# Recurrent cross attention into a three-way maxout layer, on one core: hand-written orders, bank list and queues laid out anew, state reads copied by ScalarE

## The chip, the cores and the metric

The kernel runs on one core of a Trainium2 chip. The core has five engines, each with its own instruction stream: TensorE (PE; its weight loads are shown apart as PEld), VectorE (DVE), ScalarE (ACT), GpSimd (POOL) and SyncE (SP, which here only issues DMAs). They meet through semaphores. The metric is the device time of one execution in microseconds; the median of several runs is compared. TensorE writes its results to eight banks of accumulator memory (PSUM, 2 KB per partition each); VectorE and ScalarE copy them out.

## The reference

Attention between `x` (8 batches, 8 heads, 512 positions, 64 wide) and `state` (32 positions) in both directions, then one feed-forward layer on the joined result:

```python
scores = scale * np.matmul(x, state.transpose(0, 1, 3, 2))
a = np.exp(scores - scores.max(-1, keepdims=True)); a /= a.sum(-1, keepdims=True) + 1e-09
xread = np.matmul(a, state)
scores2 = scale * np.matmul(state, x.transpose(0, 1, 3, 2))
a2 = np.exp(scores2 - scores2.max(-1, keepdims=True)); a2 /= a2.sum(-1, keepdims=True) + 1e-09
sread = np.matmul(a2, x)
tokens = np.concatenate([xread, sread], axis=2)   # then (8 * 544, 512)
h = np.maximum(np.maximum(tokens @ w1, tokens @ w2), tokens @ w3)   # 768 wide
return h @ w_out                                                    # 4352 x 512, float32
```

## The kernel before

`xread` is never formed. Since `xread @ w` is `a @ (state @ w)`, the kernel makes for each batch a matrix G (state times the three W, 2 x 128 rows by 3 x 768 columns) and multiplies the attention weights by it. Inputs are cast to bf16.

For one batch the steps are, with the short names that the order strings use:

- `lx` (or `lxg`, `lxu` by halves of the heads) loads x; `xtd` turns it by a DMA transpose on SP's queue (L245), for batches 0 and 1 `xt` on TensorE (L233) with `xtc` copying it out (L240).
- `sc` makes the scores on TensorE (L258), `ex` the exponentials on ScalarE (L265), `sum` their sums and reciprocals on VectorE (L272, L274), `wt` the product on POOL (L280); `atd` turns the weights a by DMA into aT (L298), for batches 0 and 1 `at`, `atc` on TensorE (L291, L294).
- `pad` lays x out with a column of ones on POOL (L304, L307), `sr` makes the reads of the states (L323), `srs` scales them on VectorE (L333 to L339), `srt` turns them by DMA (L342) and `ap` copies them to their place in `atp` (L347).
- `g`/`gc` make G by slices of 128 columns of each W (batches 0 and 1; L359, L377), `gr`/`grc` by runs of columns (the other batches). A run over 256 columns, or a slice, lies in a tile of two banks; `grc` copies it out at L399, whole or, with two letters, one half on each engine. A run of 256 columns lies in two tiles of one bank (`pgh`, L402).
- `l1` is one of the six slices of layer 1: six matmuls into three banks (L412). `m0` copies the first bank out on ScalarE (L427), `ma` and `mb` take the maximum with the second and third on VectorE (L432, L436). Only then are the banks free for another slice.
- `l2` is a quarter of layer 2, six matmuls into one bank (L443); `l2c` copies it out (L450), `so` stores (L473). In the last stage `l2p`, `l2pc`, `sop` do the same by parts of a quarter (L458, L462, L466), and `sos` stores rows of the state reads (L481).
- `lst`, `stc`, `stt`, `stp` load, cast, turn and place the states; `lw`, `lwo` load the weights by parts, `busy` runs matmuls on zeros, `warm` loads ScalarE's exponential.

A letter at the end of an operation is the engine that does it or the queue that issues it: D VectorE, A ScalarE, P POOL, S SyncE. Loads of x and W are issued by POOL.

Nothing reorders the work: `tc.manual_schedule()` is set, and each engine takes its instructions in the order in which three strings list the operations. FIRST has batches 0 and 1 and the start of batch 2; EACH is performed for b = 2 to 6 and holds, with indices relative to b, layer 1 and 2 of batch b and b - 1 and the attention and G of batch b + 1; LAST has batch 7, the layer for the state reads (batch "s") and the last stores. BANKS names, in order of use, which of the four single banks each single-bank tile takes, PAIRS which of the two two-bank tiles. At the end VectorE compares the sums of the exponentials with bounds (`look`, `flag`, L491 to L503), every engine reads that flag (L589), and a branch (L592) repeats the work in a safer form, which this data does not need.

```python
    for g, h in ((0, 2),) if len(c) == 1 else ((0, 1), (1, 2)):
        copier[c[g]](out=v[:, g:h], in_=p[:, g:h, 0:c1 - c0])
```

are the copies of a two-bank run.

Of the kernel before, what the change touches and what calls it, by code (L numbers as in the profile page):

```python
# [15 lines left out]


FIRST = """
    zero; busy 10; clr 3; lxu 0 0 S; lxg 1 0; lst 0 A; lxg 0 1; clr 1; busy 1; stc 0 D; clr 0; ident;
    lxg 1 1; busy 2; lw 0 2 1; stt 0; lst 1 S; cxu 0 0 D; xones 0; xt 0 0; stp 0 A; busy 2; xt 1 0;  # L20
    xtc 0 0 D; sc 0 0; busy 4; warm; xtc 1 0 D; lw 0 1 2; xt 0 1; sc 1 0; lw 0 4 0; xt 1 1; ex 0 0;
    xtc 0 1 A; sc 0 1; xones 1; sum 0 0; stc 1 P; ex 1 0; lw 1 3 2; xtc 1 1 D; lw 3 5 2; ex 0 1; lw 2 3 1;
    sum 1 0; sc 1 1; stt 1; busy 6; lw 3 6 1; lxg 2 1; wt 0 0 P; ex 1 1; at 0 0; sum 0 1; sr 0; atc 0 0 A;
    clr 2; busy 1; wt 1 0 P; stp 1 A; wt 0 1 P; at 1 0; sum 1 1; at 0 1; wt 1 1 D; g 0 0; lxg 2 0; sr 1;
    atc 0 1 A; srs 1; at 1 1; g 1 0; g 1 1; gc 0 0 A; atc 1 0 D; l1 0 0; atc 1 1 A; ones; g 0 1; gc 1 0 A;
    gc 1 1 D; m0 0 0; gc 0 1 A; xtd 2; l1 1 0; g 0 2; srs 0; m0 1 0; lw 5 6 0; g 1 2; l1 1 1; ma 0 0;
    lw 5 6 2; lw 4 5 0; l1 0 1; pad 2; mb 0 0; g 1 3; gc 0 2 A; m0 1 1; gc 1 2 A; ma 1 0; lxg 3 1; g 0 3;
    l1 0 2; m0 0 1; gc 0 3 A; m0 0 2; l1 1 2; g 0 4; mb 1 0; g 0 5; ma 1 1; l1 0 3; gc 1 3 A; lst 2 A; lwo;
    mb 1 1; l1 1 3; m0 1 2; ma 0 1; g 1 4; gc 0 4 A; g 1 5; m0 0 3; gc 0 5 A; l1 0 5; mb 0 1; ma 0 2;
    m0 1 3; mb 0 2; gc 1 4 A; m0 0 5; l1 1 4; ma 1 2; mb 1 2; ma 0 3; ma 1 3; l1 0 4; mb 0 3; mb 1 3;  # L30
    ma 0 5; mb 0 5; m0 1 4; m0 0 4; gc 1 5 A; sc 2 -; lxg 3 0; ma 1 4; mb 1 4; gr 2 1024 1280; lst 3 S;
    gr 2 0 512; ex 2 -; xtd 3; l1 1 5; ma 0 4; gr 2 512 1024; grc 2 1024 1280 D; lx 4; gr 2 1792 2304;
    mb 0 4; stc 3 P; sum 2 -; grc 2 0 512 A; grc 2 1792 2304 D; stc 2 P; l2 0 2; m0 1 5; l2 0 3;
    gr 2 1280 1792; l2c 0 2 D; wt 2 - P; stt 2; grc 2 1280 1792 A; l2 0 1; grc 2 512 1024 A; ma 1 5; mb 1 5;
    l2 0 0; stp 2 D; stt 3; sr 2; stp 3 A; l2c 0 3 D; so 0 2 4 A; l2c 0 1 D; l2c 0 0 A; srs 2; so 0 0 2 P;
    atd 2;
"""
EACH = """
    gr 1 1792 2304; lx 3; gr 1 0 512; l2 -1 3; sc 1 -; grc 1 0 512 A; pad 1; l2 -1 0; ex 1 -; l1 0 0;
    l2 -1 1; grc 1 1792 2304 D; gr 1 1280 1792; gr 1 1024 1280; srt -2; xtd 2; sum 1 -; l2c -1 3 A;  # L40
    gr 1 512 1024; sr 1; l2c -1 0 A; m0 0 0; l1 0 1; ma 0 0; l1 0 2; l2c -1 1 A; so -1 0 2 A; mb 0 0;
    grc 1 1024 1280 DA; l1 0 3; srs 1; m0 0 1; m0 0 2; ma 0 1; m0 0 3; mb 0 1; wt 1 - P; l1 0 5; m0 0 5;
    l2 -1 2; grc 1 1280 1792 A; grc 1 512 1024 A; ma 0 2; l1 0 4; mb 0 2; ma 0 3; mb 0 3; ma 0 5; m0 0 4;
    mb 0 5; ma 0 4; mb 0 4; l2c -1 2 A; atd 1; ap -2 D; so -1 2 4 P;
"""
LAST = """
    srt 7; srt 5; l1 7 0; l2 6 3; l1 7 2; ap 5 A; l2 6 1; srt 6; l1 7 3; m0 7 0; ma 7 0; mb 7 0; ap 6 A;
    ap 7 D; m0 7 2; l2c 6 3 D; l2c 6 1 A; l1 7 4; m0 7 3; l1s 0; m0 7 4; ma 7 2; mb 7 2; ma 7 3; mb 7 3;
    l1 7 1; l2 6 0; m0 s 0; ma 7 4; m0 7 1; l2c 6 0 A; ma s 0; mb 7 4; ma 7 1; mb s 0; mb 7 1; l1 7 5;
    m0 7 5; l1s 2; ma 7 5; mb 7 5; m0 s 2; l2p 7 1 384 512; l1s 1; ma s 2; l2p 7 0 384 512; l2p 7 3 256 512;  # L50
    l2pc 7 1 384 512 A; l2 6 2; m0 s 1; sop 7 1 384 512 S; l2p 7 3 0 256; ma s 1; l2p 7 2 128 384;
    l2pc 7 0 384 512 D; l1s 5; l2pc 7 3 256 512 A; l2c 6 2 A; l2p 7 0 0 128; mb s 2; l1s 3; l1s 4; mb s 1;
    l2pc 7 2 128 384 D; m0 s 5; l2p 7 2 0 128; l2p 7 2 384 512; l2p 7 0 128 256; l2pc 7 3 0 256 A;
    l2p 7 1 0 128; m0 s 3; look; ma s 5; sop 7 3 256 512 S; l2pc 7 0 0 128 D; sop 7 2 128 384 S; m0 s 4;
    sop 7 0 384 512 S; mb s 5; sop 7 0 0 128 A; ma s 3; so 6 2 3 P; so 6 1 2 S; so 6 3 4 S; so 6 0 1 P;
    l2pc 7 2 0 128 A; ma s 4; mb s 3; l2p 7 0 256 384; mb s 4; l2pc 7 0 128 256 D; flag; l2p s 0 0 256;
    l2pc 7 2 384 512 A; sop 7 0 128 256 S; sop 7 2 384 512 S; l2pc 7 1 0 128 A; l2pc 7 0 256 384 D;
    l2pc s 0 0 256 D; sop 7 2 0 128 S; l2p 7 1 128 384; l2 s 1; sop 7 1 0 128 A; l2c s 1 D;
    l2pc 7 1 128 384 A; sop 7 3 0 256 S; sop 7 0 256 384 S; sop s 0 0 256 S; sop 7 1 128 384 S;
    l2p s 0 256 512; l2pc s 0 256 512 D; sos 1 A; sop s 0 256 512 S;  # L60
"""

BANKS = """
    0123012130 2310231031 3232132013 2013210321 0321302301 3203123013 0212302131 2031203120 3123013203
    1201320132 0132013210 3120132031 2031203120 3123013203 1201320132 0132013210 3120132031 2031203120
    3123013203 1201321032 0132013021 0230213021 0320323102 3021320130 120312013
"""
PAIRS = """
    0101010110 1010100010 1010010100 1010010100 10
"""  # L70


# [1 line left out]
def kernel(  # L74
# [10 lines left out]
    nc = tc.nc  # L85

    B, H, S, D = x.shape
# [35 lines left out]
    zero = const.tile([128, 512], BF16, name="zero")  # L123
    ident = const.tile([128, 128], BF16, name="ident")
    ones = const.tile([128, 128], BF16, name="ones")
    warm = const.tile([128, 1], F32, name="warm")
# [3 lines left out]
    flag = data.tile([128, 1], I32, name="flag")  # L130

    xT, e, a, aT, G, ht, osb, xp = {}, {}, {}, {}, {}, {}, {}, {}
# [176 lines left out]
    srs = {}  # L309
# [188 lines left out]
    def set_flag():  # L498
# [3 lines left out]
        nc.vector.reduce_sum(out=n, in_=p, axis=AX.X)  # L502
        nc.vector.tensor_scalar(out=flag, in0=n, scalar1=255.5, scalar2=None, op0=ALU.is_le)  # L503

# [9 lines left out]
        "gr": (g_run, 1), "grc": (g_ran, 1), "l1": (layer1, 1), "l1s": (layer1_states, 0),  # L517
        "m0": (max_first, 1), "ma": (max_second, 1), "mb": (max_third, 1), "l2": (layer2, 1), "l2c": (layer2_out, 1),
        "l2p": (layer2_part, 1), "l2pc": (layer2_part_out, 1), "sop": (store_part, 1), "so": (store, 1), "sos": (store_states, 0), "look": (look_at_sums, 0), "flag": (set_flag, 0),
    }  # L520

    def value(t):
# [38 lines left out]
    def sread_below_max(b):  # L561
# [18 lines left out]
        for g in range(2):  # L580
            p = bank([128, 2, 2, 128], BF16, "pat")
            for c in range(2):
                for i in range(2):
# [2 lines left out]
                           in_=p.rearrange("p i c k -> p (i c) k"))  # L586
        sread(b)

    bad = nc.values_load(flag[0:1, 0:1], min_val=0, max_val=1,  # L589
                         skip_runtime_bounds_check_because="flag is the result of a comparison")  # L590
    homes["b"], homes["w"] = cycle("0123"), cycle("01")
    with tc.If(bad != 0, label="again"):  # L592
        for b in range(B):
# [68 lines left out]
```

## Time and profile before

| | us |
|---|---|
| median of 3 runs (lowest, highest) | 156.79 (156.53, 157.11) |
| span of the profiled execution | 155.3 |
| TensorE busy in it | 147.1 |
| VectorE busy | 113.6 |
| ScalarE busy | 87.1 |
| GpSimd busy | 52.1 |

The span reaches from the first to the last thing that the profiler recorded; a run's time has about 1.5 us around it. Lines of the profile give start and length in us, then engine, source line, operation, output and inputs with partitions x elements; `xN` counts instructions in a row, and a bracket gives the idle time before and what ended it. The granted TensorE clock is a share of full speed. The stretches of the windows view are columns of busy time by engine.

### The profile page before, as it was taken

Reading aid. Unit: us, or ns where it says so; the run is one execution under the profiler, and the core shown is the slowest. Engines: PE = TensorE matmul, PEld = TensorE weight load, DVE = VectorE, ACT = ScalarE, POOL = GpSimd, SP = SyncE. Lnnn points to the kernel's source line nnn. Section 1 sums busy time; section 2 is a strip of 40 time slices with the busy share of each in tenths; the row PEclk is TensorE's granted clock in tenths of the full one; section 3 lists DMA queues with packets and bytes.
Section 4 is the critical chain, followed back from the end, with each engine's and each line's share of the span. In section 5 each row is a group of like instructions: output and inputs, shape, how many; then the busy total and the mean of one; then the engine's idle time right before and its main releaser. Section 6 shows DMA issues by size and latency. Waiting matters only on the chain.

```text
span 155.3 us, 3610 instructions
## 1 busy us (share of the span) xinstructions
PE 147.1 (95%) x1429; PEld 73.6 (47%) x1429; DVE 113.6 (73%) x196; ACT 87.1 (56%) x143; POOL 52.1 (34%) x69
## 2 busy tenths in 40 slices
PE   6989899999999999999999999999999999999960
PEld 2565333354453444444444443444344445679930
DVE  3577788799957788877687799688978767636530
ACT  0677787865486476557655865466637543333300
POOL 6999509502239007700770073106220100002000
PEclk9999999999999999999999999999999999999995
DMA  4999999999979996998499930923060300015444
GB/s 123 231 196 201 196 189 171 159 189 196 194 194 224 268 151 200 130 178 163 153 128 179 177 135 0 174 44 135 4 211 17 135 2 4 0 37 202 167 145 142
DMA packets 39477, 22.30 MB, mean 144 GB/s; under 512 B 23584, under 2 KB 37408, under 8 KB 39456
## 3 DMA queue, kind: packets, MB, share of 16 engines
q0 software_dynamic: 14944, 10.75, 40.5%
q1 hardware_dynamic: 22928, 7.47, 28.2%
q10 hardware_dynamic: 1584, 3.80, 6.8%
q8 instruction: 12, 0.20, 0.5%
q14 instruction: 9, 0.07, 0.2%
HBM read 15.20 MB, written 8.91 MB: 155 GB/s over the span
## 4 chain that ended last, share of the span: by engine, by line
PE 77%; DVE 9%; DMA 6%; POOL 4%; issue 1%; DVEq 0%; POOLq 0%
PE pw L412 45%; PE po L443 19%; DMA w<-in_moe_w_dram 6%; PE pg L359 5%; PE po L458 4%; DVE atp L347 3%; DVE ht L436 2%; PE psr L323 2%; DVE seen L272 1%; DVE G L399 1%; POOL x L166 1%; PE ps L258 1%; POOL w L177 1%; DVE t L432 1%; POOL x L194 1%
## 5 line engine op out<-in xcount | busy, mean ns | idle before, releaser
L412 PE MATMUL pw<-aT,G 128*128 128x512 bf16 x288 | 67.1, 379 | 0.0
L432 DVE TENSOR_TENSOR t<-t,pw 128x512 bf16<-128x512 bf16 (+1 forms) x54 | 35.0, 649 | 14.4 <-ACT t L427 11.8
L427 ACT CAST t<-pw 128x512 bf16<-128x512 f32 (+1 forms) x54 | 30.6, 567 | 23.8 <-PE pw L412 19.9
L412 PEld LDWEIGHTS <-G 128*128 128x128 bf16 x288 | 27.2, 98 | 33.6 <-issue 2.7
L443 PE MATMUL po<-wout,ht 128*128 128x512 bf16 x168 | 40.6, 379 | 0.0
L436 DVE TENSOR_TENSOR ht<-t,pw 128x512 bf16<-128x512 bf16 x48 | 32.9, 686 | 4.8 <-PE pw L412 0.5
L473 POOL DMA_DIRECT2D out_dram<-osb x8 | 4.8, 601 | 66.1 <-ACT osb L450 43.4
L443 PEld LDWEIGHTS <-ht 128*128 128x128 bf16 x168 | 15.3, 98 | 19.3 <-issue 2.3
L399 ACT CAST G<-pg 128x1024 bf16<-128x1024 f32 x18 | 17.7, 1019 | 4.6 <-PE pg L359 4.6
L450 ACT COPY osb<-po 128x512 f32<-128x512 f32 x24 | 13.6, 589 | 10.9 <-PE po L443 10.9
L280 POOL TENSOR_TENSOR a<-e,rden 128x1024 bf16<-128x1024 bf16 (+1 forms) x9 | 14.6, 1636 | 14.4 <-DVE rden L274 6.5
L307 POOL COPY xp<-x 128x1024 bf16<-128x1024 bf16 x12 | 12.4, 1071 | 5.3 <-DMA x<-in_x_dram 5.3
L359 PE MATMUL pg<-w,bd 64*32 64x512 bf16 (+1 forms) x288 | 12.2, 364 | 0.6 <-DMA w<-in_moe_w_dram 0.6
L272 DVE TENSOR_REDUCE seen<-e 128x32 f32<-128x1024 bf16 (+1 forms) x10 | 9.9, 990 | 3.5 <-ACT e L265 3.5
L265 ACT ACTIVATE e<-ps 128x1024 bf16<-128x1024 f32 (+1 forms) x10 | 8.4, 853 | 4.0 <-PE ps L258 2.9
L377 ACT CAST G<-pg 128x768 bf16<-128x768 f32 x11 | 8.9, 808 | 2.9 <-PE pg L359 2.9
L207 PE MATMUL idle<-zero 128*128 128x512 bf16 x26 | 8.5, 472 | 1.3 <-DVE zero L185 1.3
L412 PE MATMUL pw<-atp,w 128*128 128x256 bf16 x72 | 8.7, 273 | 0.0
L359 PEld LDWEIGHTS <-bd 64*32 64x32 bf16 x336 | 3.5, 89 | 9.0 <-issue 7.6
L177 POOL DMA_DIRECT2D w<-in_moe_w_dram x10 | 7.6, 773 | 0.4 <-DMA w<-in_moe_w_dram 0.4
L412 PEld LDWEIGHTS <-w 128*128 128x128 bf16 x72 | 7.0, 98 | 1.2
L347 DVE COPY atp<-ats 128x128 bf16<-128x128 bf16 x6 | 7.5, 1254 | 0.0
(66 smaller groups left out, 111.2 us busy)
## 6 DMA issues: line engine op xcount, KB each, us to landing
out_dram<-osb ACTq DMA_DIRECT2D x6, 512.0 KB, 5.0
out_dram<-osb POOLq DMA_DIRECT2D x6, 512.0 KB, 3.0
x<-in_x_dram POOLq DMA_DIRECT2D x4, 512.0 KB, 8.1
x<-in_x_dram POOLq DMA_DIRECT2D x7, 256.0 KB, 5.9
w<-in_moe_w_dram POOLq DMA_DIRECT2D x3, 256.0 KB, 9.2
wout<-in_moe_w_out_dram POOLq DMA_DIRECT2D x1, 768.0 KB, 9.4
out_dram<-osb SPq DMA_DIRECT2D x6, 128.0 KB, 3.0
w<-in_moe_w_dram POOLq DMA_DIRECT2D x5, 128.0 KB, 8.4
```

Of the source, the lines that this page charges most:

```text
L272: nc.vector.reduce_sum(out=den, in_=parity(e[b], g), axis=AX.X)
L280: times[c](out=parity(a[b], g).rearrange("p j g s n -> p j (g s) n"), in0=parity(e[b], g).rearrange("p j g s n -> p j (g s) n"), in1=rdens ...
L307: nc.gpsimd.tensor_copy(out=xp[b][:, :, :, g * (D + 1):g * (D + 1) + D], in_=v[:, g])
L347: copier[c](out=atp[:, :, b // 4, :, b % 4], in_=ats[:, b])
L359: nc.tensor.matmul(p(s, g), bd(b, 2 * s + g)[64 * g:64 * g + 64, g, :], f(w_sb[64 * g:64 * g + 64, s]), start=True, stop=True, tile_positi ...
L399: copier[c[g]](out=v[:, g:h], in_=p[:, g:h, 0:c1 - c0])
L412: nc.tensor.matmul(pw[i][:, 0:n], lhs(i, k), rhs(k), start=(k == 0), stop=(k == nk - 1))
L427: nc.scalar.copy(out=t0s[b, m][:, 0:n], in_=open_ps["l", b, m][0][:, 0:n])
L432: nc.vector.tensor_max(t1s[b, m][:, 0:n], t0s.pop((b, m))[:, 0:n], open_ps["l", b, m][1][:, 0:n])
L436: nc.vector.tensor_max(ht[b][:, m, :], t1s.pop((b, m))[:, 0:n], open_ps.pop(("l", b, m))[2][:, 0:n])
L443: nc.tensor.matmul(p, ht[b][:, m, j * 128:(j + 1) * 128], wout_sb[:, m, :], start=(m == 0), stop=(m == NM - 1))
L450: copier[c[i]](out=o[:, j, i * w:i * w + w], in_=p[:, i * w:i * w + w])
```

## The change

Only orders, the bank and pair lists and one small function change; what is computed stays. The passes:

```diff
 EACH = """
-    gr 1 1792 2304; lx 3; gr 1 0 512; l2 -1 3; sc 1 -; grc 1 0 512 A; pad 1; l2 -1 0; ex 1 -; l1 0 0;
-    l2 -1 1; grc 1 1792 2304 D; gr 1 1280 1792; gr 1 1024 1280; srt -2; xtd 2; sum 1 -; l2c -1 3 A;
-    gr 1 512 1024; sr 1; l2c -1 0 A; m0 0 0; l1 0 1; ma 0 0; l1 0 2; l2c -1 1 A; so -1 0 2 A; mb 0 0;
-    grc 1 1024 1280 DA; l1 0 3; srs 1; m0 0 1; m0 0 2; ma 0 1; m0 0 3; mb 0 1; wt 1 - P; l1 0 5; m0 0 5;
-    l2 -1 2; grc 1 1280 1792 A; grc 1 512 1024 A; ma 0 2; l1 0 4; mb 0 2; ma 0 3; mb 0 3; ma 0 5; m0 0 4;
-    mb 0 5; ma 0 4; mb 0 4; l2c -1 2 A; atd 1; ap -2 D; so -1 2 4 P;
+    pad 1; l2 -1 0; gr 1 1792 2304; gr 1 1024 1280; l2c -1 0 A; grc 1 1024 1280 DA; gr 1 0 512; l1 0 0;
+    l2 -1 3; l1 0 1; m0 0 0; ma 0 0; sc 1 -; grc 1 0 512 AD; m0 0 1; mb 0 0; grc 1 1792 2304 AD; ma 0 1;
+    l2 -1 1; l1 0 2; ex 1 -; sr 1; l2c -1 1 A; mb 0 1; gr 1 1280 1792; gr 1 512 1024; l1 0 3; m0 0 2;
+    so -1 0 2 A; srt -2; l1 0 5; l1 0 4; sum 1 -; m0 0 3; m0 0 5; l2 -1 2; l2c -1 3 D; ma 0 2; srs 1;
+    mb 0 2; ma 0 3; m0 0 4; mb 0 3; ma 0 5; mb 0 5; grc 1 512 1024 DA; wt 1 - P; ap -2 A; ma 0 4;
+    mb 0 4; l2c -1 2 D; so -1 2 4 P; lx 3; xtd 2; grc 1 1280 1792 A; atd 1;
 """
```

In a pass, the load of x and its transpose move to the end, three runs of G are copied by halves (one on ScalarE, one on VectorE), two of the four copies of layer 2 move from ScalarE to VectorE, and the copy of the state reads moves from VectorE to ScalarE. In FIRST and LAST (cut):

```diff
 FIRST = """
-    zero; busy 10; clr 3; lxu 0 0 S; lxg 1 0; lst 0 A; lxg 0 1; clr 1; busy 1; stc 0 D; clr 0; ident;
...
+    lxg 0 1; lxg 1 0; zero; clr 0; busy 1; busy 2; lxu 0 0 S; clr 1; ident; busy 1; lxg 1 1; busy 1;
+    busy 1; busy 1; lst 0 A; stc 0 D; busy 1; busy 1; stt 0; xones 1; cxu 0 0 D; stp 0 D; xt 0 0;
+    busy 1; lw 0 4 0; xtc 0 0 A; lw 0 1 2; busy 2; busy 1; xones 0; xt 0 1; busy 2; xtc 0 1 D; sc 0 0;
+    ex 0 0; xt 1 0; sc 0 1; lst 1 S; busy 1; busy 1; busy 1; xtc 1 0 AD; xt 1 1; busy 1; ex 0 1;
+    sum 0 0; sum 0 1; busy 1; xtc 1 1 AD; lw 0 2 1; lw 1 3 2; sc 1 0; lw 2 3 1; busy 1; sr 0; sc 1 1;
+    busy 1; ex 1 0; ex 1 1; busy 1; wt 0 0 P; at 0 0; busy 2; sum 1 0; wt 0 1 P; sum 1 1; wt 1 0 P;
+    busy 2; at 0 1; atc 0 0 A; at 1 0; lw 5 6 0; srs 0; busy 1; stc 1 A; stt 1; g 1 0; wt 1 1 D;
+    lw 5 6 2; lw 3 5 2; atc 0 1 A; g 0 0; lw 3 6 1; at 1 1; sr 1; atc 1 0 A; gc 1 0 D; g 0 1; g 1 1;
+    srs 1; gc 0 0 A; l1 0 0; gc 0 1 D; lw 4 5 0; atc 1 1 A; gc 1 1 A; stp 1 DA; m0 0 0; g 0 2; g 1 2;
...
+    ma 1 2; gc 1 4 AD; g 0 5; xtd 2; m0 0 3; g 1 5; l1 1 3; mb 1 2; gc 0 5 A; l1 0 5; m0 1 3; ma 0 3;
...
+    grc 2 1024 1280 AD; l2 0 2; m0 1 5; gr 2 0 512; xtd 3; srs 2; gr 2 1792 2304; so 0 0 2 P;
+    grc 2 512 1024 AD; ma 1 5; atd 2; stp 3 AD; mb 1 5; l2c 0 2 D; grc 2 1792 2304 A; grc 2 0 512 DA;
+    lx 4; so 0 2 4 S;
 """
...
 LAST = """
-    srt 7; srt 5; l1 7 0; l2 6 3; l1 7 2; ap 5 A; l2 6 1; srt 6; l1 7 3; m0 7 0; ma 7 0; mb 7 0; ap 6 A;
...
-    l2p s 0 256 512; l2pc s 0 256 512 D; sos 1 A; sop s 0 256 512 S;
+    l1 7 2; srt 5; ap 5 D; l1 7 0; srt 6; l1 7 3; m0 7 2; m0 7 0; srt 7; l1 7 4; ap 6 A; ma 7 2; mb 7 2;
...
+    l2p s 0 256 512; sop 7 2 128 384 P; sop 7 3 256 512 A; sos 1 A; l2pc 7 0 128 256 D;
+    l2pc s 0 256 512 A; sop s 0 0 256 P; sop s 0 256 512 A; l2pc 7 0 384 512 D; vl; sop 7 0 384 512 P;
+    sop 7 0 128 256 S;
 """
...
+    bads = []
+
+    def read_flag():
+        bads.append(nc.values_load(flag[0:1, 0:1], min_val=0, max_val=1,
+                                   skip_runtime_bounds_check_because="flag is the result of a comparison"))
...
+        "vl": (read_flag, 0),
...
-    bad = nc.values_load(flag[0:1, 0:1], min_val=0, max_val=1,
-                         skip_runtime_bounds_check_because="flag is the result of a comparison")
+    bad = bads[0]
```

In FIRST the G slices, layer 1 slices and maxima of batches 0 and 1 stand next to each other slice by slice, the weights are loaded in another order, the warm-up matmuls are 28 instead of 26 in more and smaller groups, and some copies go to another engine. In LAST the layer 2 parts and stores come in another order, POOL and ScalarE issue more of the stores (all DMAs: ScalarE 15 for 11, POOL 34 for 30, SyncE 9 for 17), and the flag is read ahead of the last two stores (`vl`).

## The prediction

> **What bounds it now.** I read the page's busy shares, then the chain of waits, then the busy time of each engine cut at the passes (cut points are the starts of the first G run of each pass), then the timeline where a pass is long.
>
> ```profile
> PE 147.1 (95%) x1429; PEld 73.6 (47%) x1429; DVE 113.6 (73%) x196; ACT 87.1 (56%) x143; POOL 52.1 (34%) x69
> ```
>
> TensorE works in 95% of the span and no other engine comes near. The change leaves its matmuls alone (1429 against 1431), so a gain can come only from its waits, the head (first slice of layer 1 starts at 17.02) and the tail. The passes, columns being length, then busy time of PE, PEld, DVE, ACT, POOL:
>
> ```profile
> 43.60:58.85 15.25, 15.25 (x157) 6.89 (x164) 10.72 (x19) 10.76 (x18) 5.48 (x6) 1.00 1.21 216
> 58.85:74.10 15.25, 15.25 (x157) 6.83 (x164) 12.36 (x20) 9.70 (x16) 5.61 (x6) 1.00 0.95 170
> 74.10:89.35 15.25, 15.25 (x157) 6.84 (x164) 11.56 (x20) 9.70 (x16) 5.51 (x6) 1.00 0.88 159
> 89.35:105.51 16.16, 15.88 (x156) 6.80 (x164) 13.32 (x20) 9.70 (x16) 4.63 (x5) 1.00 0.39 85
> ```
>
> Three passes are pure TensorE work, 15.25 each at clock 1.00. The fourth is 0.91 longer with the same work. The chain of waits (start, length, what) shows why, and the timeline (start, length, engine, line, operation) shows what the long piece is:
>
> ```profile
> 89.35 0.60 PE pg L359 x16
> 89.95 0.67 DVE ht L436
> 90.62 2.16 DVE atp L347
> 92.78 1.04 DVE G L399
> ```
> ```profile
> 75.29 0.30 DVE L347 COPY atp<-ats 128x128 bf16<-128x128 bf16 x1
> ...
> 90.54 2.24 DVE L347 COPY atp<-ats 128x128 bf16<-128x128 bf16 x1
> 90.56 2.05 POOL L307 COPY xp<-x 128x1024 bf16<-128x1024 bf16 x2
> ...
> 96.66 0.42 DVE L402 CAST G<-pgh 128x256 bf16<-128x256 f32 x1
> 96.69 0.37 ACT L402 CAST G<-pgh 128x256 bf16<-128x256 f32 x1 [0.41 <-PE pgh L359]
> ```
>
> The same small VectorE copy takes 0.30 alone and 2.24 beside POOL's padding copies; VectorE then runs late and TensorE waits for banks. It happens again at 106.7, costing about 0.44. So the waits in the passes come to 0.91 + 0.44 = 1.35 us: all that the passes have to give.
>
> **The change, part by part.**
>
> *State reads copied by ScalarE (ap).* The VectorE copies of 2.13 to 2.24 go; ScalarE's two of this kind take 0.486 each. No row has one beside POOL's copies: from 0.49 (ScalarE's other copies there, 0.59 and 1.01, keep their usual time) to 2.24. I take 0.49; ScalarE is busy 9.7 of 15.25. Gain 1.35. At 2.24, up to 1.75 a pass, ScalarE's idle time still covers it.
>
> *Halves.* In EACH three of the four two-bank G pieces (0-512, 1792-2304, 512-1024) are now copied half by ScalarE and half by VectorE ("AD", "DA"). By sizes the pair looks like 0.59 and 0.68 side by side in place of 1.02. But the program as built has, on the second engine's copy, a wait on the first engine's counter, since both read one two-bank tile; the 256-wide pieces, two separate tiles, have none, and the rows at 96.66 and 96.69 run together. So a split piece takes 0.59 + 0.68 = 1.27 in series, where the whole took 1.02 on ScalarE (two of the three) or 1.21 on VectorE (1792-2304). What is queued behind the second copy waits too: VectorE's max operations, which free layer 1's banks.
>
> *VectorE also gets* two of four layer 2 copies (0.684 each) and loses the atp copy. By rows a pass of VectorE is 12 max operations 8.20, three halves 2.05, a 256 half 0.42, sum 1.57, two layer 2 copies 1.37, state-read scaling 0.46: 14.07, where it had 10.7 to 12.4. That still fits a pass; the order decides.
>
> *Order in a pass.* T = 0 is the start of layer 1's slice 1. Its first bank is done at 0.59, ScalarE's m0 runs 0.69-1.28, its half of 1792-2304 1.18-1.76 (an engine starts its next work some 0.1 before the last ends), VectorE's half 1.80-2.49, then ma 2.40-3.08 and mb 3.18-3.87. TensorE, after layer 2 of the batch before and the scores, wants slice 2's banks at 3.05: it waits 0.08 and 0.36. Next on VectorE: the reduction 3.79-5.00, reciprocal 5.04-5.39, layer 2 copy 5.31-6.00, ma of slice 2 5.91-6.59. TensorE wants slice 3 at 5.79: 0.48 in three waits. The last mb ends at 12.37 and the next pass begins with a layer 2 that needs it: 0.18. Together 1.10 a pass, for five passes 5.5. In the first place VectorE's half waits for ScalarE's; the layer 2 copy in the second is one that ScalarE had.
>
> *Entry to the passes.* VectorE does two ma/mb pairs in a row (0.68 + 0.69 + 0.69 + 0.69) ahead of its half of the 0-512 piece of batch 2, and ScalarE's half waits behind that: TensorE wants the pair's banks at 45.69 and gets them at 46.67, 0.98, with 0.19 before it. In the last stage the same form costs 0.10 and 0.58 (m0 7 2 behind a half, an ap 0.49 and a G copy 1.02). Entry and end: 1.85.
>
> *Head.* The x part of batch 0 that needs a cast still lands at 4.90 and the cast ends at 5.63. From there: transposes to 6.37, ScalarE's copy (1.01 where VectorE takes 0.69) to 7.42, second half copied by 8.41, scores 8.63, exps to 8.98; batch 1's xT halves in series (0.58, then 0.41), exps, the first sum to 10.48, its reciprocal to 10.77. POOL's three products:
>
> ```profile
> 11.13 3.10 POOL L280 TENSOR_TENSOR a<-e,rden 128x512 bf16<-128x512 bf16 x3
> ...
> 16.73 0.36 PE L359 MATMUL pg<-w,bd 64*32 64x384 bf16 x8 [0.59 <-DMA w<-in_moe_w_dram]
> ```
>
> run 10.91-14.07 instead, and transposes with a state turn (0.22) put the first G at 14.96, before 14.61: +0.35. After that the slices of both batches stand side by side and wait for halves (placing of states, gc 1 4) and banks: 0.36, 0.28, 0.09, 0.09, 0.08 and 0.36, and 0.2 for the second G piece of batch 0: 1.46 to 1.6 where before had 0.92 (0.59 of it the wait for W in the row above, which the new W order removes or not: 0 to 0.59). I carry +1.1 at batch 2's scores. Warm-up matmuls (26 to 28) lie in time in which TensorE waits anyway; the VectorE/ScalarE chain of the head hides them, and uncovered they would be 2 x 0.47.
>
> *Fewer G visits and a moved state turn* save TensorE 0.36 of switching (entering a G visit costs 0.09, leaving about 0.3, by gaps between rows).
>
> *Tail.* Before, POOL's last store is issued by 141.6 and landed at 143.98, and SP's last is issued at 151.06, 1.8 behind the last matmul group's start:
>
> ```profile
> 149.28 0.82 PE L458 MATMUL po<-wout,hts 128*128 128x256 bf16 x6
> ...
> 151.06 0.56 SPq L466 DMA_DIRECT2D out_dram<-osb  x1
> ```
>
> Now POOL issues stores to the very end. POOL's closing steps, in the trace's raw records, start when its stores have landed: 0.79 and a drain of 2.51, hidden before. Last store issued about 0.3 behind the last copy, landing 2 later, 0.1 + 0.79 + 0.03 + 2.51 + 0.83: 6.6 to 7.1 from the last matmul's start to the end, before 155.30 - 149.82 = 5.48: +1.2 (0 if the drain overlaps the landings, +1.6 at most). The flag's read, ahead of the last two stores, lies beside the waits for copies: nothing, at most one store's issue, 0.6.
>
> **Sum**: +1.1 (head) + 5.5 + 1.85 (waits) - 1.35 - 0.36 = +6.8 for the last matmul; +1.2 tail; +8.0. The profiled span of 155.3 becomes 163.3. The median of the runs, 156.79, has 1.5 outside that span: 164.8.
>
> **Rivals.**
>
> (A) *The halves run side by side*, the wait being satisfied early or absent. For: the rows at 96.66 and 96.69. Against: the built wait, 18 such halves. With the half at 0.68 beside 0.59, five passes and the entry lose about 5.2 less: 159.6. The Trainium skill, PSUM — Partial Sum Buffer, section "PSUM bank collisions raise a hardware error", has two engines on different banks run clean, which speaks for the chip not needing this wait; by that rule alone the time would be this rival's, but the program's wait is there whatever the chip needs.
>
> (B) *The DMA chain x, xT, a, aT becomes the bound.* The load of x and the transposing DMA move to the end of the pass. In my pass the sum ends at 5.39, POOL's product (1.91) at 7.4, and aT is wanted about 13.85: 6.4 for a transfer whose rows land in 2.7 to 5.95; at 5.4 with its issue there is 0.85 to spare. Landing 1.5 later costs (1.5 - 0.85) x 5.5 = 3.6: 168.4. For: rows near 6. Against: less DMA traffic on SP (9 issues against 17). The Trainium skill, SBUF — State Buffer, section "Who interferes with whom", says a VectorE copy can hold up POOL's making of descriptors; more VectorE copies and 34 POOL DMAs against 30 would push this way, and no row here shows an issue so stretched.
>
> (C) *Faster*: VectorE's lag stays inside the bank slack (TensorE never waits in the passes), the 1.35 goes, the 0.36 too, and head and tail come out even: 156.79 - 1.71 = 155.1. It decides if VectorE's half and the max behind it end before 3.05 in the pass, which needs halves side by side and the reduction elsewhere. For: three passes had no wait at 12.36 of VectorE work. Against: 14.07 of it now.
>
> That the change does nothing measurable: the head's and tail's losses just meet the 1.35. It needs (C)'s passes too.
>
> **How the numbers follow.** Forecast 0.62 (its own range 162 to 167.5: tail 0 to 1.6, head 0.5 to 1.5, a pass 0.7 to 1.5); A 0.17; B 0.12; C 0.06; even 0.03. A measurement here can tell 0.5%, 0.8 us, from no change. Faster 0.06, same 0.03, slower 0.91. The range must reach A at 159.6 and half of B: 159.5 to 168.5, leaving out C, even and B's upper half, some 0.15.
>
> **What would show it.** Passes near 16.3, all alike, with TensorE waiting for ma, mb; "AD" copies ending one behind the other; atp copies of 0.5 on ScalarE; first G near 15.0; the span's end 6.6 or more behind the last matmul. It is wrong if passes stay near 15.3 (A, C), if TensorE waits for aT by DMA (B), or if POOL's end is hidden again.

## The result, and the profile after

The changed kernel takes 167.38 us (median of 4, 166.84 to 167.87), the kernel before 156.83 in the same comparison: ratio 1.0666, 95% interval 1.0634 to 1.0697. It is slower by 10.5 us, and the spans of the two profiled executions differ by as much (165.77 - 155.30 = 10.47). All ratios rest on the faster executions of a kernel, and the profiled ones of three kernels further on (separate banks, whole copies, last POOL stores on SyncE) lie 1.5% or more above the fastest of theirs. The busy shares of the page after:

```profile
PE 150.1 (91%) x1415; PEld 73.7 (44%) x1431; DVE 118.7 (72%) x217; ACT 81.5 (49%) x143; POOL 53.6 (32%) x72
```

TensorE's share falls from 95% to 91%: the work is the same and the waits have grown. Its busy time still rises, from 147.1 to 150.1, because the record of a layer matmul lasts 0.38 while the next one usually starts 0.22 behind it: the first 0.16 of a wait counts as busy. Two marks that both traces have, the start of batch 2's scores and the start of the last matmul, cut the loss in three:

| stretch (us) | before | after | difference | in the prediction's sum |
|---|---|---|---|---|
| to batch 2's scores | 33.93 | 37.18 | +3.25 | +1.1 |
| from there to the last matmul | 115.89 | 120.26 | +4.37 | 5.5 + 1.85 - 1.35 - 0.36 = +5.64 |
| from there to the end of the span | 5.48 | 8.33 | +2.85 | +1.2 |

The windows view, cut at the scores of four passes after the change (length; busy time of PE, PEld, DVE, ACT, POOL; clock; DMA share; GB/s):

```profile
53.32:69.46 16.14, 15.78 (x149) 6.79 (x148) 12.91 (x22) 8.76 (x16) 5.51 (x6) 1.00 0.58 126
69.46:85.60 16.14, 15.73 (x147) 6.78 (x148) 12.91 (x22) 8.70 (x16) 5.51 (x6) 1.00 0.78 148
85.60:101.74 16.14, 15.73 (x147) 6.80 (x148) 12.91 (x22) 8.71 (x16) 5.51 (x6) 1.00 0.83 150
101.74:117.96 16.22, 15.75 (x148) 6.80 (x149) 12.91 (x22) 8.72 (x16) 4.62 (x5) 1.00 0.62 142
```

Three of these are 16.14 and the last is 16.22, at full clock: at least 0.89 more than the 15.25 of an undisturbed pass before, though no engine is full. The chain of waits in one of them (start, length, what):

```profile
68.33 0.45 PE pw L415 x2
...
68.85 0.58 ACT t L430
69.44 0.50 ACT G L402
...
69.96 0.69 DVE G L402
70.65 0.60 DVE t L435
...
71.35 0.69 DVE ht L439
72.03 1.14 DVE seen L275
...
73.47 0.64 DVE osb L453
...
74.15 3.99 PE pw L415 x17
```

For 5.3 us the chain leaves TensorE: ScalarE's m0 and its half of a G run, then VectorE's half, which starts as ScalarE's ends, then the maxima, the sum and the layer 2 copy that VectorE got, until a bank comes free at 74.11. TensorE has other work for most of that time, but not for all of it: by the starts of its matmuls it loses 0.44 at layer 1's slice 2 and 0.33 at slice 3. A third and smaller wait stands in the first layer 2 of the next pass, which needs the last mb:

```profile
80.50 0.11 PEld L446 LDWEIGHTS <-ht 128*128 128x128 bf16 x2 [0.49 <-DVE ht L439]
```

The two matmuls around it start 0.38 apart and not 0.22: 0.16.

At the head the timeline has a wait that the kernel before has not, on a transfer:

```profile
27.07 4.43 SPq L248 DMA_TRANSPOSE xT<-x  x1
...
37.18 0.64 PE L261 MATMUL ps<-bd,xT 128*128 128x64 bf16 x16 [1.55 <-DMA xT<-x]
```

Further on stands the wait that the prediction has at the entry to the passes, for the pair of banks whose second half ScalarE copies after VectorE:

```profile
49.08 0.41 PE L362 MATMUL pg<-w,bd 64*32 64x512 bf16 x8 [0.97 <-ACT G L402]
```

### The profile page after: what moved, and what is told of

The parts are those of the page before. It is cut to its first block, busy times and chain, and to the rows that moved or that the text cites. A ratio compares the mean times of both kernels' runs of the same rounds, so it can differ in the third digit from the quotient of the medians.

```text
span 165.8 us, 3624 instructions
## 1 busy us (share of the span) xinstructions
PE 150.1 (91%) x1415; PEld 73.7 (44%) x1431; DVE 118.7 (72%) x217; ACT 81.5 (49%) x143; POOL 53.6 (32%) x72
## 4 chain that ended last, share of the span: by engine, by line
PE 50%; DMA 14%; DVE 14%; ACT 8%; POOL 5%; issue 4%; POOLq 0%; DVEq 0%; ACTq 0%; SPq 0%
PE pw L415 28%; PE po L446 14%; DMA xT<-x 6%; DMA x<-in_x_dram 5%; DVE G L402 3%; ACT G L402 3%; DVE ht L439 2%; DMA osb<-in_x_dram 2%; ACT t L430 2%; DVE osb L453 2%; POOL w L180 2%; DVE t L435 2%; DVE seen L275 2%; PE po L461 2%; PE pg L362 2%
## 5 line engine op out<-in xcount | busy, mean ns | idle before, releaser
L415 PE MATMUL pw<-aT,G 128*128 128x512 bf16 x288 | 69.8, 379 | 2.6 <-DVE ht L439 1.2
L446 PE MATMUL po<-wout,ht 128*128 128x512 bf16 x154 | 39.7, 379 | 0.7
L402 ACT CAST G<-pg 128x512 bf16<-128x512 f32 (+1 forms) x24 | 17.6, 733 | 7.4 <-DVE G L402 6.1
L402 DVE CAST G<-pg 128x512 bf16<-128x512 f32 x17 | 11.7, 685 | 7.2 <-ACT G L402 7.2
L476 POOL DMA_DIRECT2D out_dram<-osb x7 | 4.3, 609 | 30.9 <-DVE osb L453 18.9
L362 PE MATMUL pg<-w,bd 64*32 64x512 bf16 (+1 forms) x288 | 11.5, 364 | 1.0 <-ACT G L402 1.0
L453 DVE COPY osb<-po 128x512 f32<-128x512 f32 x15 | 10.0, 666 | 3.2 <-PE po L446 3.2
L453 ACT COPY osb<-po 128x512 f32<-128x512 f32 x14 | 8.1, 586 | 8.2 <-PE po L446 8.2
L210 PE MATMUL idle<-zero 128*128 128x512 bf16 x26 | 9.0, 466 | 1.4 <-DVE zero L188 1.3
L471 POOL DMA_DIRECT2D out_dram<-osb x4 | 2.2, 540 | 22.8 <-ACT osb L465 21.7
```

The costliest lines, as they stand in the source:

```text
L362: nc.tensor.matmul(p(s, g), bd(b, 2 * s + g)[64 * g:64 * g + 64, g, :], f(w_sb[64 * g:64 * g + 64, s]), start=True, stop=True, tile_positi ...
L415: nc.tensor.matmul(pw[i][:, 0:n], lhs(i, k), rhs(k), start=(k == 0), stop=(k == nk - 1))
L446: nc.tensor.matmul(p, ht[b][:, m, j * 128:(j + 1) * 128], wout_sb[:, m, :], start=(m == 0), stop=(m == NM - 1))
L453: copier[c[i]](out=o[:, j, i * w:i * w + w], in_=p[:, i * w:i * w + w])
```

## The experiments

Each of the twelve kernels below was timed beside the kernel before. "Ratio" is to that, with its 95% interval, and a time given with a ratio is the ratio times 156.83. The wait for the head's transfer is 0.9 to 3.9 in the profiles of the kernels that keep it, and the three named above had 2.9 to 3.9. So a part is read from its own stretch of the trace as well: scores of batch 2 to last matmul is 120.26 in the changed kernel.

**Separate banks for the halves.** Each two-bank tile becomes two tiles of one bank (orders and engines stay; scores, slices and runs of G likewise). With that, a whole copy of two banks becomes two copies, and the exponentials go in two instructions:

```diff
-    def two_banks(shape, dtype, name):
-        return pp.tile(shape, dtype, tag="w" + next(homes["w"]), bufs=1, name=name)
+    def two_tiles(shape, dtype, name):
+        w = next(homes["w"])
+        return [pp.tile(shape, dtype, tag=f"w{w}{h}", bufs=1, name=f"{name}{h}") for h in range(2)]
```

> The changed kernel (167.4) with each two-bank tile replaced by two tiles of one bank, so that a half on the second engine no longer waits for the half on the first; same engines, same orders (the exponentials go in two instructions). Theory S (the wait between the two halves, in series, is most of the loss in the passes): TensorE's first stall of a pass (0.44) goes and the second shrinks, passes 16.14 become about 15.4, the 0.97 at the entry goes: 162 to 163. Rival V (the copies that VectorE got, by their mere length and order, are the loss): halves overlap in the trace, but the passes stay above 15.9 and the time at 166 or more.

Measured: ratio 1.0262 (1.0226 to 1.0297), 160.9 on 156.83. Passes 15.36, TensorE's list of waits empty from 54 to 116; scores to last matmul 116.40. One pass, and the halves in its timeline:

```profile
70.01:85.37 15.36, 15.26 (x147) 6.81 (x148) 13.10 (x23) 8.72 (x18) 5.51 (x6) 1.00 0.82 156
```

```profile
53.87 0.68 DVE L410 CAST G<-pg 128x512 bf16<-128x512 f32 x1
54.04 0.59 ACT L435 CAST t<-pw 128x512 bf16<-128x512 f32 x1 [1.52 <-PE pw L420]
54.52 0.59 ACT L410 CAST G<-pg 128x512 bf16<-128x512 f32 x1
```

VectorE copies its half while ScalarE is still busy with m0, and no longer waits for ScalarE's. VectorE is as busy in a pass as in the changed kernel (13.1, there 12.9), so it is not its load by itself that cost. Theory S holds, and V falls. The stretch is 3.86 shorter, the time 6.4. The rest is not in the passes. A shorter wait at the head in the executions behind the ratio would give at most 1.55 of it, and the tail in the trace is 0.27 shorter; some 0.8 stays open, and no trace of those executions is at hand.

**Whole copies in the passes.** The same question from the other side:

```diff
-grc 1 0 512 AD; ... grc 1 1792 2304 AD; ... grc 1 512 1024 DA;
+grc 1 0 512 A;  ... grc 1 1792 2304 D;  ... grc 1 512 1024 A;
```

> The changed kernel with the three split runs of G in a pass copied whole again by the engines of before (0-512 and 512-1024 ScalarE, 1792-2304 VectorE), nothing else. Theory S: VectorE's copy no longer waits 1.2 for ScalarE, its first max starts 0.65 earlier, both stalls of a pass (0.4 each) go: passes 15.3 to 15.4, entry wait stays: about 163.3. Rival V: VectorE loses 0.84 of 14 us a pass and no more than that can come back; if the layer 2 copy on VectorE is what holds the banks, one stall of 0.4 stays: passes 15.7 to 15.8, 165.3.

Measured: ratio 1.0326 (1.0274 to 1.0378), 161.9. Passes 15.27, scores to last matmul 115.42, 4.84 less than the changed kernel and 0.47 less than before the change; the entry's 0.97 stays. One pass:

```profile
72.01:87.28 15.27, 15.16 (x147) 6.82 (x148) 12.41 (x21) 8.96 (x14) 5.51 (x6) 1.00 0.83 157
```

VectorE still has its two layer 2 copies of a pass here, so the stall behind them needs the late start that the halves cause. Whole copies do better in this stretch than halves in separate tiles (115.42 against 116.40, there with every whole copy in two as well): here the split wins nothing even when its halves need not wait for each other.

**Layer 2 copies on ScalarE again**, one of them further ahead in the order.

```diff
-l2c -1 1 A; ... l2c -1 3 D; ... l2c -1 2 D;
+l2c -1 3 A; l2c -1 1 A; ...     l2c -1 2 A;
```

> The changed kernel with VectorE's two layer 2 copies of a pass on ScalarE again. Theory S: the second stall of a pass (0.4, behind VectorE's layer 2 copy) goes, the first (behind the serial halves) stays: passes 15.7, about 165.2. Rival V: both go, passes 15.3, about 163.

Measured: ratio 1.0705 (1.0632 to 1.0777), no gain in time; the scores of batch 2 came at 38.30 in its profile, 1.1 later than in the changed kernel's. In the trace the passes are 15.86: 0.28 less, where S said 0.4 and V 0.8.

```profile
70.30:86.17 15.87, 15.57 (x148) 6.89 (x149) 11.82 (x20) 9.44 (x18) 5.51 (x6) 1.00 0.82 152
```

The timeline has the same wait between the halves as the changed kernel, and the first stall; no wait for VectorE's layer 2 copy is left in the list of waits of the passes:

```profile
86.67 0.69 DVE L402 CAST G<-pg 128x512 bf16<-128x512 f32 x1 [1.19 <-ACT G L402]
...
88.80 1.02 PE L415 MATMUL pw<-aT,G 128*128 128x512 bf16 x4 [0.20 <-DVE ht L439]
```

So it points to S, with a smaller second stall than worked out: the layer 2 copies on VectorE cost 0.28 a pass, and only behind the serial halves. Scores of batch 2 to last matmul took 119.16, 1.10 less; in the profiled execution the head took as much, and the times don't show it.

**x of batch 2 loaded early.** POOL's queue, behind the first three products:

```diff
-at 1 0; lw 5 6 0; ... lw 5 6 2; lw 3 5 2; ... lw 3 6 1; ... lw 4 5 0; ... lxg 2 1; mb 0 0; lxg 2 0;
+lw 3 5 2; lw 3 6 1; lw 4 5 0; lxg 2 1; lxg 2 0; lw 5 6 0; lw 5 6 2;
```

> The changed kernel with the load of x of batch 2 put before two parts of W in POOL's queue (behind the first three products), so that it lands about 2 to 3 us earlier. Theory D (scores of batch 2 wait 1.55 for the turned x, because its load stands behind five loads of W and its transpose then runs beside the load of the output weights for 10 us): the transpose starts near 24, lands by 34 to 35, the wait goes: 165.8, with scores of batch 2 near 35.6. Rival: behind that wait is another of the same length, a bank that VectorE or ScalarE holds, and the time stays within 0.5 of 167.4.

Measured: ratio 1.0572 (1.0544 to 1.0600), 165.8; scores of batch 2 at 35.38. Theory D holds to 0.3, though the transpose took 9.4 here too: what helped is that it began 2.5 earlier. The four times lie within 0.53 of each other.

**Last POOL stores on SyncE.**

```diff
-so 6 1 2 P; ... sop 7 0 0 128 P; ... sop 7 2 128 384 P; ... sop s 0 0 256 P; ... sop 7 0 384 512 P;
+so 6 1 2 S; ... sop 7 0 0 128 S; ... sop 7 2 128 384 S; ... sop s 0 0 256 S; ... sop 7 0 384 512 S;
```

> The changed kernel with the last five stores that POOL issues moved to SyncE's queue. Theory P (POOL ends with about 0.87 and a drain of 2.84 that start only when its last store has landed, exposed here): from the last matmul's start to the span's end 8.4 becomes 5.5, as before the change: 164.5. Rival F (reading the flag ahead of the last stores delays them): the end stays 7 or more behind the last matmul, 166.5 or more.

Measured: from the last matmul to the end 5.39, against 8.33: theory P holds to 0.1. The ratio, 1.0546 (1.0480 to 1.0612), shows 1.9 less and not 2.9, with a wide interval: in its profiled execution the scores of batch 2 waited 3.9 for the head's transfer.

**Flag read last.** `vl` is put behind the last store.

> The changed kernel with the flag read behind the last two stores instead of ahead of them. Theory P: nothing, within 0.4 of 167.4. Rival F: 1 us or more is won.

Measured: ratio 1.0720 (1.0685 to 1.0755), the end 8.32 behind the last matmul. Nothing is won, and F falls.

**x and its transpose in the front half of a pass.**

```diff
-so -1 2 4 P; lx 3; xtd 2; grc 1 1280 1792 A;
+lx 3; l1 0 1; ... srt -2; xtd 2; l1 0 5; ... so -1 2 4 P; grc 1 1280 1792 A;
```

> The changed kernel with the load of x and its transpose put back into the front half of a pass. Theory: they have time to spare in the passes either way, within 0.4 of 167.4. Rival B (the chain of DMAs bounds the passes): 1 us or more is won.

Measured: ratio 1.0641 (1.0584 to 1.0698), passes 16.14, scores to last matmul 120.28. Nothing: rival B falls for the passes.

**Before, last store on POOL.** `sop s 0 256 512` by POOL instead of SyncE.

> The kernel before with its very last store issued by POOL instead of SyncE, nothing else. Theory P: POOL's closing steps become exposed, plus 2.5 to 3: 159.5. Rival: POOL's store only takes the place of one that SyncE issued later, plus 0.5 or less.

Measured: ratio 1.0258 (1.0234 to 1.0283), 4.0 us; the end 9.40 behind the last matmul, against 5.48. Theory P, and more than it said:

```profile
151.21 0.56 POOL L466 DMA_DIRECT2D out_dram<-osb  x1 [9.30 <-DVE osb L462]
```

This one store landed only at 155.1, 3.9 behind its issue; in the trace's raw records POOL's closing step of 0.81 and drain of 2.59 followed, to 158.7.

**Before, state reads copied by ScalarE.** `ap -2 D` becomes `ap -2 A` in EACH.

> The kernel before with the state reads of a pass copied by ScalarE instead of VectorE, nothing else. Theory: the copies of 2.1 to 2.2 beside POOL's padding copies become 0.5, the pass that had 16.16 takes 15.25 and the wait behind it goes: 1.35 less, 155.5, which beats both kernels. Rival: ScalarE's copy is stretched to 2 by POOL as VectorE's was, and delays its m0: less than 0.5 won.

Measured: ratio 0.9890 (0.9868 to 0.9913), 155.1 on 156.83, and a faster kernel than both. From batch 3 on the distances between scores are 15.24 to 15.25 throughout, scores to last matmul 114.67, 1.22 less. The copies take 0.49:

```profile
L347 ACT COPY atp<-ats x7: 477/491/553, 58.3 to 120.4; 128x128 bf16<-128x128 bf16 x7
```

(number of them, then shortest, median and longest in ns). The view of one pass has the copy at 88.84, where VectorE's stood at 90.54, and POOL's padding copies only from 89.92. In no run here does ScalarE's copy stand beside them, so the rival's stretched copy is untested: the gain may come from the earlier place as much as from the other engine.

**The same, and one store moved.** `sop 7 1 128 384` of the last stage by ScalarE, two places further ahead.

> As the one above, and one store of the last stage moved from SyncE's queue to ScalarE's and further ahead, so that SyncE is free when the last copy ends (before: copy ends 150.55, store issued 151.06). Theory: 0.4 less again, 155.1. Rival: another store or the flag's read on SyncE ends last: as the one above, within 0.3.

Measured: ratio 0.9867 (0.9843 to 0.9891), 154.7; the end 5.08 behind the last matmul, against 5.49 in the run above. The theory's 0.4 is in the trace; the intervals overlap, so the times alone don't settle it.

**Three parts undone together**, then with the last G run of the head whole as well (`grc 2 0 512 DA` becomes `A`).

> The changed kernel with three of the parts above undone together: whole copies in the passes, x of batch 2 loaded early, the last POOL stores on SyncE. If the account of the loss is whole, the gains add: scores of batch 2 at 35.4, 115.4 from there to the last matmul, 5.4 behind it: span 156.2, time 157.7 to 158. If one mechanism was hiding another, it stays 1.5 or more above that.

> As the one above, and the last G run of the head (0-512 of batch 2) copied whole by ScalarE. Theory S: TensorE's wait of 0.97 for that pair of banks shrinks by about 0.8: 157. Rival: ScalarE, with the copy of 1792-2304 ahead of it, gives the banks no earlier: no change.

Measured: ratio 1.0072 (1.0040 to 1.0103), 158.0, as expected: scores of batch 2 at 35.89, 115.63 to the last matmul, 5.85 behind it. Then 1.0055 (1.0031 to 1.0078), 157.7: the wait at the entry falls from 0.97 to 0.16 and the distance from the scores of batch 2 to the next from 16.35 to 15.53, 0.82 as theory S says. The times show 0.3, inside their intervals. What is left above the kernel before (0.9) is the head's: scores of batch 2 at 35.66 are 1.73 later, the middle stretch (114.83) is 1.06 shorter, the tail (5.79) 0.31 longer, together +0.98.

## Why the prediction was right or wrong

*The direction and the largest term were right.* Counted from 68.16, where layer 1's slice 1 starts, the steps of the chain above end at 1.27, 1.78, 2.49, 3.09, 3.88, 5.01 and 5.95, each within 0.05 of the working. Of its stalls the first was 0.44, as worked out, and the third 0.16 (0.18); the second was 0.33 and not 0.48. Together they are near the 0.89 that a pass has more, where 1.10 was worked out, so five passes at 0.89 cost 4.45 and not 5.5. That is most of the 1.27 by which the middle stretch came out smaller; of the rest, some 0.35 lies in terms that no run measured apart (the last stage, the switching of TensorE).

One reading in the working is uneven: its 14.07 of VectorE work in a pass is a sum of durations, set beside 10.7 to 12.4 of busy time. Neighbouring rows overlap by about 0.1, and the busy time after the change is 12.91. So VectorE had more room than that comparison says, and the order decided, as the working has it.

*The entry* was worked out as 0.98 and measured as 0.97.

*The state reads* were priced at a gain of 1.35. Done alone on the kernel before they gave 1.22 in the trace and 1.1% of the time (1.7 us, interval 1.4 to 2.1): 0.92 in the pass with the late copy, as read, and 0.30 behind it, where 0.44 was taken. That ScalarE's copy keeps its 0.49 beside POOL's padding copies was a choice without a row; the case never came up, which is luck.

*Rival A* supposed that halves run side by side and priced this at 159.6. With separate banks they need not wait for each other, and it is 160.9. In the changed kernel they do wait: the wait is in the program, one tile to its bookkeeping. The Trainium skill, PSUM — Partial Sum Buffer, section "PSUM bank collisions raise a hardware error", has engines on different banks run clean. The experiment agrees that the chip needs no such wait: there VectorE's half runs ahead of ScalarE's, each from its bank.

*The step that failed is the head's +1.1.* It was the lag of the copies and sums alone, and that part was near: the first G came at 15.04 where 14.96 was worked out, and without the wait for x the scores of batch 2 come at 35.38, +1.45. What the head's sum left out is the load of x of batch 2. The prediction moved W's loads and saw the chain x, xT only in the passes (rival B). In POOL's queue x stands behind five loads of W after the products, is issued at 17.88 and 18.61 instead of 10.37 and 14.15, and lands at 26.99 instead of 23.16. Its transpose then runs beside two other loads of POOL's, which were both issued behind it before: the output weights, which land at 31.63, and x of batch 3, which lands at 36.02 and 37.49. The rows before and after, and the time from issue to landing of that transpose:

```profile
23.24 2.05 SPq L245 DMA_TRANSPOSE xT<-x  x1
...
25.93 0.83 POOL L182 DMA_DIRECT2D wout<-in_moe_w_out_dram  x1
```
```profile
DMA to landing us min/median/max: 5.0/5.0/5.0
```
```profile
17.88 1.54 POOL L169 DMA_DIRECT2D x<-in_x_dram  x2
19.34 0.90 POOL L185 DMA_DIRECT2D wout<-in_moe_w_out_dram  x1
...
27.07 4.43 SPq L248 DMA_TRANSPOSE xT<-x  x1
28.23 1.50 POOL L169 DMA_DIRECT2D x<-in_x_dram  x2
```
```profile
DMA to landing us min/median/max: 10.1/10.1/10.1
```

Of the transpose's 2048 packets the first starts 2.13 behind its issue (before: 1.31) and the last 7.79 behind it (before: 3.96). It lands at 37.13, and TensorE, which wants it at 35.6, waits 1.55: most of the 2.15 that the head's term was short. The Trainium skill, DMA: Bandwidth & Descriptors, section "Issuing engines are not separate DMA queues", says that transfers issued by different engines share the same 16 DMA engines and interleave. The rows agree: SyncE's transpose is slow where POOL's loads are in flight. No run takes one of these loads away, so which of them slows it, and by how much, is not shown. The experiment with x loaded early shows only that the wait is gone when the transpose begins 2.5 sooner. So rival B's mechanism was right, its place wrong.

*The tail* was +1.2, measured +2.85: the mechanism right, its size off. POOL's last store:

```profile
157.88 0.54 POOL L471 DMA_DIRECT2D out_dram<-osb  x1 [1.18 <-DVE osb L465]
```

It was issued 0.44 behind the last matmul's start and 0.30 behind its copy, as taken. It landed 3.26 later (2 taken), and the closing step and drain took 0.87 and 2.84 (0.79 and 2.51 taken). The bound of 1.6 was too low mainly because the landing was priced at 2, near the low end of the last stores before (1.60 to 3.87). The flag's read costs nothing, as said.

So the sum's +8.0 (7.94 by its terms) was 10.5: +2.15 too little at the head and +1.65 at the tail, -1.27 too much between. The time fell inside the range, near its top; that the middle was priced too high and took 1.27 off the miss is luck.

## What to carry to other kernels

Two halves of one tile, copied by two engines, were serial here, and everything that stood behind the second half on its engine was late. Look at the waits in the built program before pricing halves as parallel, and compare with the whole copy: here it gave the shortest passes (15.27, against 15.36 and 16.14 with halves). When loads in a queue are reordered, follow each moved load to its first reader, and ask what its transfer will now run beside. Let no store issued by GpSimd be the last thing of a kernel: here that cost 2.9 to 4.0 us.

## What the runs showed of the hardware

The end of GpSimd's queue is dear: one last store there cost the kernel before 4.0 us (3.9 from issue to landing, 0.81 to close, a drain of 2.59).

A DMA transpose of one batch's x landed 5.0 after its issue when the output weights and the next batch's x were loaded behind it, and 9.3 to 12.5 when it met these loads (12.5 in the run with the last stores on SyncE); in the changed kernel and the variants that keep its loads, scores of batch 2 started anywhere from 37.2 to 40.6. With x loaded earlier the transpose still took 9.4 and 9.7, but ended in time, and they started at 35.4 to 35.9. The times of one kernel lie 1.0 to 5.1 apart in the seven with the late load of x and 0.5 to 1.2 apart in the three with the early one; that this transfer makes the spread is likely, but only one execution of each was traced.

VectorE's small copy of the state reads takes 0.30 alone and 2.13 to 2.24 beside POOL's padding copies (three of each kind in the kernel before). ScalarE's took 0.48 to 0.56, never beside those.
